# VectorE's evacuation moved ahead of the reciprocal, and the second head mixing run three steps behind the first, in a talking-heads attention with an MLP behind it

## Chip, cores and metric

One core of a Trainium2 chip runs the whole program. The metric is the device time of one launch in microseconds (us); the median of three runs is compared. The core has five engines that work side by side, each through its own instructions in order: TensorE (PE, its weight loads are PEld), VectorE (DVE), ScalarE (ACT), GpSimd (POOL) and SyncE (SP), which here only issues DMA transfers. They wait for one another by semaphores.

## The reference

```python
scores = scale * np.matmul(q, k.transpose(0, 1, 3, 2))        # 4 batches, 12 heads, 448 x 448
scores = np.einsum('bhij,hg->bgij', scores, w_pre)             # first mixing of the heads
scores = scores - np.max(scores, axis=-1, keepdims=True)
attn = np.exp(scores)
attn = attn / (np.sum(attn, axis=-1, keepdims=True) + 1e-09)
attn = np.einsum('bhij,hg->bgij', attn, w_post)                # second mixing
x = np.matmul(attn, v)                                         # -> 1792 tokens x 768
h = x @ w_in                                                   # 768 x 2048
r = np.maximum(h, 0.0)
out = (s * (r * r) + b) @ w_out                                # 2048 x 768
```

## The kernel before

**Blocks and steps.** The queries of a batch are cut into 4 chunks, 16 chunks in all, and each chunk into 11 or 12 blocks of up to 10 queries. A block holds 10 queries x 12 heads = 120 partitions by 448 keys, so that mixing the heads is one matrix product with a 120 x 120 matrix. There are 180 blocks, and one loop over steps `s` (lines 755 to 784) works on several blocks at once, each at another stage.

**What a step does, in the order in which it is written.** `relayout(s + 5)` fetches a block's scores by DMA, and `split(s + 2)` cuts them on GpSimd into a high and a low part. From step 12 on, `convert_step` issues one of the seven VectorE instructions that turn a piece of the MLP's weights into two float parts; seven such pieces are made during the attention, which is 49 steps, 12 to 60. `normalize(s - 1)` takes the reciprocal of the sums (VectorE, L566) and writes the high half of the normalized weights, tile `eh`, on ScalarE (L568). `low_parts()` issues the VectorE subtractions (L233) that are queued in the list `later`. `evacuate(s - 3)` copies the second mixing's result from PSUM (tile `po`) to tile `A` (VectorE L606, ScalarE L604 in the last chunk). `premix(s)` is three matmuls into `pm` (L547), the row maximum (VectorE L549), the exponential with its sum (ScalarE L554) and a small scaling of the sum (ScalarE L558). `remainder(s - 1)` is VectorE L575: the low half of `eh`. `postmix(s - 2)` is the second mixing, twelve matmuls (L590) with `eh` as weights.

**The work between.** A plan that is made ahead (lines 616 to 691) hands each step some of the other work: `prep_q` and `prep_k` (transposes on PE, a copy on ScalarE L443 or L423, and a subtraction for `low_parts`), `qk_pair` (scores of two heads: six matmuls L464, one ScalarE copy L474), `av_pair` (attention times v, L488), loads of q, k and v, and, in the last chunk, pieces of the MLP's first product (`head_piece`, L248). `FILL`, `QK_COST` and `AV_COST` spread the pairs over the steps. A step carries a `prep`, a `qk_pair`, an `av_pair`, both pairs, or nothing. No `qk_pair` stands in a step with a `prep`. In the last chunk (blocks 168 to 179) `split_x` gives six steps a ScalarE copy (L224) and a VectorE subtraction of the MLP's input.

**What keeps the stages apart.** Tiles have a fixed number of buffers: `pm` three PSUM banks together with `px` (two in the last chunk), `po` two, `eh` two, `Tk` (the transposed keys) eight. After step 182 comes the MLP, which the change doesn't touch.

Of the kernel before, what the change touches and what calls it, by code (L numbers as in the profile page):

```python
# [21 lines left out]
def talking_heads_attention__then__act_relu2_kernel(  # L22
# [160 lines left out]
    def convert_step(upto):  # L183

        if done["run"] is None:
            if done["conv"] >= min(upto, len(units)):
                return False
            done["run"] = conversion(done["conv"])
        try:
            next(done["run"])  # L190
        except StopIteration:
            done["run"] = None
            done["conv"] += 1
        return True
# [216 lines left out]
    def prep_k(b, p):  # L411
        low_parts()
        nat = nat_t.pop((b, p))
        tr = bank(f"trk_{b}_{p}") if b == 0 else ps.tile([P, 2, 512], F32, tag="sc", name=f"trk_{b}_{p}")[:, 0]
        for c in range(NC):
            n = P if c < NC - 1 else KL
            nc.tensor.transpose(
                tr[:, c * P:c * P + n],
                nat[:n, c].rearrange("p h d -> p (h d)"),
                ident[:n, :n],  # L420
            )
        t = qkp.tile([P, 2, S], F32R, tag="Tk", name=f"Tk_{b}_{p}", bufs=8)
        nc.scalar.activation(t[:, 0, :], tr[:, :S], AF.Copy)  # L423
        later.append((t[:, 1, :], tr[:, :S], t[:, 0, :]))
        k_t[b, p] = t
# [136 lines left out]
    def normalize(t):  # L562

        n = blocks[t][2] * H
        e, st = e_t[t]
        nc.vector.reciprocal(st[:n, 3:4], st[:n, 2:3])  # L566
        eh = blkp.tile([BP, 2, S], F16, tag="eh", name=f"eh_{t}", bufs=2)
        nc.scalar.activation(eh[:n, 0, :], e[:n], AF.Copy, scale=st[:n, 3:4])  # L568
        eh_t[t] = eh

# [75 lines left out]
            fill.append((when, lo, w1 - 1, QK_COST, 1, qk_pair, (ci, p)))  # L646
    for ci in range(NCH):
        b = chunks[ci][0]
        w0 = first[ci + 1] + 3
        w1 = first[ci + 2] + 3 if ci + 2 <= NCH else NB + 100  # L650
        if ci == NCH - 1:
            w0 = NB + 3
        for p in range(NP):
            when = w0 + p * min(w1 - w0, 12) / NP
            fill.append((when, w0, w1 - 1, AV_COST, 1, av_pair, (ci, p)))
            if b + 1 < B and chunks[ci + 1][0] != b:
                at(w0 + (p + 1) * (w1 - w0) / NP, 2, load_v, b + 1, p)
    w0 = first[NCH - 1] + 3
    for i in range(NHEAD * NKC):
        if i < NHEAD * NKC - LATE:  # L660
            when = w0 + i * (NB + 3 - w0) / (NHEAD * NKC - LATE)
            fill.append((when, w0, NB + 2, 0.567, 1, head_piece, ()))
        else:
            fill.append((NB + 100, NB + 3, NB + 100, 0.567, 1, head_piece, ()))
    fill.sort(key=lambda x: x[0])
    spent, closed = 0.0, {}
    for s in range(NB + 4):
        spent = max(spent, -0.4) + load.get(s, 0)
        left, held = [], set()
        for x in fill:  # L670
            _, lo, hi, cost, order, f, args = x
            waits = f in held

            opens = f is qk_pair or (f is av_pair and args[1] % 4 == 0)
            if opens and closed.get(f, -1) >= s and s <= NB + 2 and s < hi:
                waits = True

            if f is qk_pair and s in load and s < hi:
                waits = True
            if not waits and lo <= s and (s > NB + 2 or hi <= s or (x[0] < s + 4 and spent < FILL)):  # L680
                at(s, order, f, *args)
                spent += cost
                if f is qk_pair or (f is av_pair and args[1] in (3, NP - 1)):
                    closed[f] = s
            else:
                held.add(f)
                left.append(x)
        fill = left
        spent -= FILL
# [62 lines left out]
        x[3](*x[4])  # L752
        low_parts()
    tail = first[NCH - 1]
    for s in range(NB + 3):
        if s == tail - LD:
            early.close()
            rp = ctx.enter_context(tc.tile_pool(name="rp", bufs=1, side="right", reuse_waits="tile"))
            for n in range(NU_EARLY, NU_EARLY + NU_TAIL):
                w_pool[n] = rp  # L760
        if s + LD < NB:
            relayout(s + LD)
        if s + LS < NB:
            split(s + LS)
        if 0 <= s - 1 < NB:
            if s >= CONV0:
                convert_step(NU_EARLY)
            normalize(s - 1)
        low_parts()
        if 0 <= s - 3 < NB:  # L770
            evacuate(s - 3)
        if s < NB:
            premix(s)
        if 0 <= s - 1 < NB:
            remainder(s - 1)
        run_plan(s, True)
        if 0 <= s - 2 < NB:
            postmix(s - 2)
        run_plan(s, False)
        if 0 <= s - (tail - LD) < NKC:  # L780
            load_x(0, 0, s - (tail - LD))
        if 0 <= s - tail < NKC:
            split_x(0, 0, s - tail)
            load_x(0, 1, s - tail)
# [100 lines left out]
```

## Time and profile before

| | |
|---|---|
| median of three runs | 1003.28 us (1002.81 to 1005.6) |
| the profiled execution | 1006.37 us, its span 1004.7 us |
| busy share PE / PEld / DVE / ACT / POOL | 94% / 80% / 64% / 61% / 39% |
| mean granted TensorE clock | 0.98 |
| attention / MLP | up to about 520 us / from there on |

The span is what lies between the first and the last instruction on the core; 1.7 us of the execution lie around it. The chain of waits gives, at each moment, the work that the end hung on; over the span it goes 52% through PE, 21% through ACT and 18% through DVE. Most of PE's share is the MLP.

### The profile page before, as it was taken

The page shows a single profiled execution, that of the slowest core. Times are in us where ns is not written, and L with a number is a line of the kernel's source. Part 1 is how long each engine was busy: PE and PEld are TensorE (multiplying, and loading weights), DVE is VectorE, ACT ScalarE, POOL GpSimd, SP SyncE. Part 2 cuts the span into 40 slices and gives each one's busy share as a digit, 9 for nine tenths or more (in the row PEclk, how much of TensorE's full clock was granted, in tenths as well). Part 3 has the DMA queues.
Part 4 walks back from the last instruction along what each step waited for, and adds up shares of the span by engine and source line. Part 5 has one row for each costly group of instructions (what it writes and reads, how often), then busy time and mean ns, then how long its engine had stood idle before and what let it go on. Part 6 is the DMA issues. An engine that isn't in the chain of part 4 may idle for free.

```text
span 1004.7 us, 19819 instructions
## 1 busy us (share of the span) xinstructions
PE 942.6 (94%) x7500; PEld 799.3 (80%) x7500; DVE 641.9 (64%) x1314; ACT 608.1 (61%) x1315; POOL 393.8 (39%) x458
## 2 busy tenths in 40 slices
PE   5699999989999999999897999899999999999998
PEld 3466677767777677777686999799999899999998
DVE  2679999967877778888636704918542931757411
ACT  2477788868887788887666788612214687821000
POOL 0376667666677566767512333200001333310000
PEclk9889999999999999999798999899999999999999
DMA  3655444664346543544411412314450240145521
GB/s 85 163 134 134 122 144 126 171 158 119 107 121 154 146 129 99 143 126 137 150 30 47 150 56 71 95 63 137 139 177 31 92 142 1 48 126 182 158 95 55
DMA packets 127922, 114.63 MB, mean 114 GB/s; under 512 B 66770, under 2 KB 123730, under 8 KB 127826
## 3 DMA queue, kind: packets, MB, share of 16 engines
q1 hardware_dynamic: 119762, 102.35, 36.8%
q10 hardware_dynamic: 8064, 11.01, 3.0%
q8 instruction: 59, 0.97, 0.4%
q14 instruction: 37, 0.30, 0.1%
HBM read 58.28 MB, written 16.52 MB: 74 GB/s over the span
## 4 chain that ended last, share of the span: by engine, by line
PE 52%; ACT 21%; DVE 18%; DMA 4%; issue 2%; SPq 2%; POOL 0%; ACTq 0%; DVEq 0%; POOLq 0%
PE po L300 23%; PE ph L248 16%; ACT pm L554 7%; ACT S L474 5%; DVE st L549 4%; PE xp L488 4%; PE pm L547 3%; DVE A L606 3%; ACT eh L568 3%; PE sc L464 3%; ACT st L558 2%; PE po L590 2%; DMA blk<-S 2%; DVE eh L575 2%; DVE Tq L233 1%
## 5 line engine op out<-in xcount | busy, mean ns | idle before, releaser
L300 PE MATMUL po<-w,g 128*128 128x384 f32 x1344 | 237.2, 339 | 5.4 <-ACT h L256 5.4
L300 PEld LDWEIGHTS po<-w,g 128*128 128x128 f32 x1344 | 236.2, 190 | 6.0 <-ACT h L256 6.0
L535 POOL TENSOR_TENSOR hl<-blk,hl 120x448 fp32r<-120x448 f32 x180 | 206.8, 1149 | 15.0
L266 POOL TENSOR_TENSOR g<-h,g 128x448 fp32r<-128x448 f32 x64 | 79.1, 1237 | 303.6 <-ACT g L265 291.9
L534 POOL TENSOR_SCALAR hl<-blk 120x448 fp32r<-120x448 f32 x180 | 104.3, 579 | 176.9 <-PE pm L547 131.8
L248 PE MATMUL ph<-x,w 128*128 128x448 f32 x810 | 166.2, 365 | 0.0
L590 PEld LDWEIGHTS <-eh 120*128 120x128 f16 (+1 forms) x2160 | 118.0, 99 | 55.6 <-DVE eh L575 26.0
L248 PEld LDWEIGHTS ph<-x,w 128*128 128x128 f32 x810 | 152.0, 188 | 12.1
L590 PE MATMUL po<-wpost,eh 120*128 120x120 f16 (+1 forms) x2160 | 148.2, 220 | 10.1 <-DVE eh L575 9.9
L554 ACT ACTIVATE pm<-pm,st 120x448 f32<-120x448 f32 x180 | 109.6, 609 | 79.2 <-DVE st L549 78.1
L575 DVE SCALAR_TENSOR_TENSOR eh<-pm,st,eh 120x448 f16<-120x448 f32 x180 | 122.2, 679 | 14.4 <-ACT eh L568 10.5
L549 DVE TENSOR_REDUCE st<-pm 120x1 f32<-120x448 f32 x180 | 111.0, 617 | 15.2 <-PE pm L547 14.6
L568 ACT ACTIVATE eh<-pm,st 120x448 f16<-120x448 f32 x180 | 114.2, 634 | 10.4 <-DVE st L566 10.2
L606 DVE COPY A<-po 128x480 f32<-128x480 f32 x168 | 107.4, 639 | 0.0
L547 PE MATMUL pm<-hl,wpre_hi 120*120 120x448 f32 x360 | 104.2, 371 | 1.2 <-POOL hl L535 1.2
L464 PE MATMUL sc<-Tk,Tq 64*110 64x448 f32 (+1 forms) x576 | 87.4, 412 | 13.7 <-DVE Tk L233 4.8
L488 PE MATMUL xp<-A,v 128*64 128x110 f32 (+1 forms) x1536 | 93.0, 267 | 1.0 <-ACT xs L502 1.0
L154 ACT ACTIVATE mk<-raw 128x384 f32<-128x384 f32 x64 | 35.4, 553 | 95.8 <-DMA raw<-in_moe_w_out_dram 34.0
L474 ACT ACTIVATE S<-sc 110x896 f32<-110x896 f32 (+1 forms) x90 | 82.0, 911 | 13.6 <-PE sc L464 10.1
L488 PEld LDWEIGHTS xp<-A,v 128*64 128x64 f32 x1536 | 75.4, 138 | 16.0 <-issue 8.9
L547 PE MATMUL pm<-hl,wpre_lo 120*120 120x448 f32 x180 | 84.0, 467 | 3.6 <-DVE eh L575 3.1
L547 PEld LDWEIGHTS pm<-hl,wpre_hi 120*120 120x120 f32 x360 | 66.9, 186 | 6.3 <-POOL hl L535 2.0
(64 smaller groups left out, 968.6 us busy)
## 6 DMA issues: line engine op xcount, KB each, us to landing
blk<-S SPq DMA_DIRECT2D x172, 210.0 KB
raw<-in_moe_w_in_dram SPq DMA_DIRECT2D x32, 384.0 KB
raw<-in_moe_w_out_dram SPq DMA_DIRECT2D x32, 384.0 KB
xraw<-xd SPq DMA_DIRECT2D x48, 224.0 KB
part<-ob ACTq DMA_DIRECT2D x28, 192.0 KB
acc<-part SPq DMA_DIRECT2D x28, 192.0 KB
out_dram<-acc ACTq DMA_DIRECT2D x28, 192.0 KB
nk<-in_k_dram SPq DMA_DIRECT2D x48, 96.0 KB
```

The lines of the kernel that those rows point to most:

```text
L248: nc.tensor.matmul(ph[:, :S], w[:, i, c0:c0 + P], x[:, y, :], start=(kc == 0 and m == 0), stop=(kc == NKC - 1 and m == 2),)
L300: nc.tensor.matmul(po[:, :NO], g[:, x, c0:c0 + P], w[:, y, :], start=(f == 0 and m == 0), stop=(f == NF - 1 and m == 2),)
L474: nc.scalar.activation(s_t[ci][:n, 2 * p:2 * p + 2, :], x_t["two"][:n, :, :S], AF.Copy, scale=SCALE)
L488: nc.tensor.matmul(xp[e * D:(e + 1) * D, p % 4, :n], vt[:, e, c, :], a[:, c, 2 * p + e, :n], start=(c == 0), stop=(c == NC - 1),)
L535: nc.gpsimd.tensor_tensor(out=hl[:n, 1, :], in0=blk[:n], in1=hl[:n, 0, :].bitcast(F32), op=ALU.subtract)
L547: nc.tensor.matmul(pm[:n, :S], w[:n, :n], hl[:n, x, :], start=(m == 0), stop=(m == 2))
L549: nc.vector.tensor_reduce(out=st[:n, 0:1], in_=pm[:n, :S], axis=AX.X, op=ALU.max, negate=True)
L554: nc.scalar.activation(e[:n], e[:n], AF.Exp, bias=st[:n, 0:1], accum_out=pm[:n, S:S + 1])
L568: nc.scalar.activation(eh[:n, 0, :], e[:n], AF.Copy, scale=st[:n, 3:4])
L575: nc.vector.scalar_tensor_tensor(out=eh[:n, 1, :], in0=e[:n], scalar=st[:n, 3:4], in1=eh[:n, 0, :], op0=ALU.mult, op1=ALU.subtract,)
L590: nc.tensor.matmul(po[:, c * BP:(c + 1) * BP], eh[:n, x, j0:j0 + P], wpost[:n, y].rearrange("p g i -> p (g i)"), start=(m == 0), stop=(m = ...
L606: nc.vector.tensor_copy(dst, src)
```

## The change

VectorE's order within a step changes. `low_parts` and `evacuate` now stand ahead of `normalize`, so that the reciprocal of a block comes behind the copy to `A`, and the row maximum follows the reciprocal directly. `convert_step` moves from the head of the step to behind `remainder`. `postmix` works on block `s - 3` in place of `s - 2`, and `evacuate` on `s - 4` in place of `s - 3`. The loop has one more step, `eh` a third buffer, and `Tk` seven buffers in place of eight. In the plan, all `av_pair`s and the loads of v that hang on them come one step later, and the head pieces start at the last chunk's fourth step at the earliest.

```diff
-        t = qkp.tile([P, 2, S], F32R, tag="Tk", name=f"Tk_{b}_{p}", bufs=8)
+        t = qkp.tile([P, 2, S], F32R, tag="Tk", name=f"Tk_{b}_{p}", bufs=7)
...
-        eh = blkp.tile([BP, 2, S], F16, tag="eh", name=f"eh_{t}", bufs=2)
+        eh = blkp.tile([BP, 2, S], F16, tag="eh", name=f"eh_{t}", bufs=3)
...
-        w0 = first[ci + 1] + 3
+        w0 = first[ci + 1] + 4
...
-            when = w0 + i * (NB + 3 - w0) / (NHEAD * NKC - LATE)
-            fill.append((when, w0, NB + 2, 0.567, 1, head_piece, ()))
+            when = w0 + i * (NB + 4 - w0) / (NHEAD * NKC - LATE)
+            lo = first[NCH - 1] + max(4, 2 + min(i, NKC - 1))
+            fill.append((when, lo, NB + 3, 0.567, 1, head_piece, ()))
...
-    for s in range(NB + 3):
+    for s in range(NB + 4):
...
+        low_parts()
+        if 0 <= s - 4 < NB:
+            evacuate(s - 4)
         if 0 <= s - 1 < NB:
-            if s >= CONV0:
-                convert_step(NU_EARLY)
             normalize(s - 1)
-        low_parts()
-        if 0 <= s - 3 < NB:
-            evacuate(s - 3)
         if s < NB:
             premix(s)
         if 0 <= s - 1 < NB:
             remainder(s - 1)
+            if s >= CONV0:
+                convert_step(NU_EARLY)
         run_plan(s, True)
-        if 0 <= s - 2 < NB:
-            postmix(s - 2)
+        if 0 <= s - 3 < NB:
+            postmix(s - 3)
```

On VectorE, two steps in a row around blocks 23 to 26, where weights are converted (the rows on `u`, `w` and `raw`). The number behind a name is the block's. Before:

```order
L575 SCALAR_TENSOR_TENSOR eh_23_1369<-pm_23_1333,st_23_1337,eh_23_1369 120x448
L178 SCALAR_TENSOR_TENSOR w_1_1150<-raw_1_330,u_1_1152 128x384
L566 RECIPROCAL st_24_1377<-st_24_1377 120x1
L606 COPY A_2_1382<-po_22_1383 128x48x10
L549 TENSOR_REDUCE st_25_1420<-pm_25_1416 120x1
L575 SCALAR_TENSOR_TENSOR eh_24_1413<-pm_24_1373,st_24_1377,eh_24_1413 120x448
L155 TENSOR_SCALAR u_2_1463<-raw_2_1098 128x384
L566 RECIPROCAL st_25_1420<-st_25_1420 120x1
```

The same engine and blocks in the changed kernel:

```order
L575 SCALAR_TENSOR_TENSOR eh_23_1356<-pm_23_1318,st_23_1322,eh_23_1356 120x448
L176 TENSOR_SCALAR u_1_1142<-w_1_1140 128x384
L606 COPY A_1_909<-po_21_1368 128x48x10
L566 RECIPROCAL st_24_1362<-st_24_1362 120x1
L549 TENSOR_REDUCE st_25_1402<-pm_25_1398 120x1
L575 SCALAR_TENSOR_TENSOR eh_24_1396<-pm_24_1358,st_24_1362,eh_24_1396 120x448
L178 SCALAR_TENSOR_TENSOR w_1_1140<-raw_1_330,u_1_1142 128x384
L606 COPY A_2_1410<-po_22_1411 128x48x10
```

The copy to `A` went from behind the reciprocal to ahead of it, so that only the row maximum (L549) stands between a block's reciprocal (L566) and its remainder (L575).

On VectorE in a step that follows a `prep` (here of `Tq`, line L233). Before:

```order
L159 SCALAR_TENSOR_TENSOR u_2_1463<-raw_2_1098,u_2_1463 128x384
L566 RECIPROCAL st_26_1474<-st_26_1474 120x1
L233 TENSOR_TENSOR Tq_4_1492<-trq_4_0_1493,Tq_4_1492 128x4x110
L606 COPY A_2_1382<-po_24_1479 128x48x10
L549 TENSOR_REDUCE st_27_1522<-pm_27_1518 120x1
```

In the changed kernel:

```order
L155 TENSOR_SCALAR u_2_1452<-raw_2_1088 128x384
L233 TENSOR_TENSOR Tq_4_1468<-trq_4_0_1469,Tq_4_1468 128x4x110
L606 COPY A_2_1410<-po_23_1455 128x48x10
L566 RECIPROCAL st_26_1474<-st_26_1474 120x1
L549 TENSOR_REDUCE st_27_1507<-pm_27_1503 120x1
```

The subtraction and the copy both stand ahead of the reciprocal now.

On PE, the matmuls between two second mixings at block 27. Before:

```order
L439 MATMUL trq_4_0_1493<-ident_124,nq_4_1205 128x110 x4
L488 MATMUL xp_1_0_1446<-A_1_891,v_0_1_404 64x110 x8
L547 MATMUL pm_27_1518<-hl_27_1406,wpre_lo_126 120x448
L547 MATMUL pm_27_1518<-hl_27_1406,wpre_hi_125 120x448 x2
L590 LDWEIGHTS eh_25_1467
```

In the changed kernel:

```order
L439 MATMUL trq_4_0_1469<-ident_124,nq_4_1182 128x110 x4
L488 MATMUL xp_1_0_1475<-A_1_909,v_0_0_400 64x110 x8
L488 MATMUL xp_1_0_1475<-A_1_909,v_0_1_404 64x110 x8
L547 MATMUL pm_27_1503<-hl_27_1391,wpre_lo_126 120x448
L547 MATMUL pm_27_1503<-hl_27_1391,wpre_hi_125 120x448 x2
L590 LDWEIGHTS eh_24_1396
```

The second mixing behind block 27's first takes block 24 in place of 25.

## Rows read from the trace of the kernel before

**Rows 1.** Busy time of each engine in three stretches: the conversion steps, the later attention, and ten microseconds of the last chunk. Columns: stretch in us, its length, then busy us (number of instructions) of PE, PEld, DVE, ACT and POOL, granted TensorE clock, DMA share, GB/s.

```profile
80.00:210.00 130.00, 121.83 (x1352) 89.77 (x1350) 119.35 (x254) 102.92 (x249) 85.94 (x103) 1.00 0.53 142
235.00:470.00 235.00, 228.67 (x2566) 169.85 (x2566) 188.23 (x393) 191.79 (x463) 158.69 (x197) 1.00 0.47 126
480.00:490.00 10.00, 6.88 (x51) 5.38 (x48) 7.41 (x15) 6.88 (x18) 3.86 (x5) 0.61 0.56 177
```

**Rows 2.** Groups of instructions in 80 to 210 us, VectorE. Columns: line, engine, operation, tiles, shapes, count, busy us and mean ns of one, then the idle time of the engine just before them and what ended it.

```profile
L575 DVE SCALAR_TENSOR_TENSOR eh<-pm,st,eh 120x448 f16<-120x448 f32 (+1 forms) x48 | 32.6, 678 | 3.2 <-ACT eh L568 2.5
...
L566 DVE RECIPROCAL st<-st 120x1 f32<-120x1 f32 (+1 forms) x48 | 7.6, 159 | 3.4 <-ACT st L558 3.1
```

**Rows 3.** The same view of 235 to 470 us: the reciprocal, and PE's second mixing.

```profile
L590 PE MATMUL po<-wpost,eh 120*128 120x120 f16 (+1 forms) x1104 | 74.0, 217 | 2.4 <-DVE eh L575 2.3
...
L566 DVE RECIPROCAL st<-st 120x1 f32<-120x1 f32 (+1 forms) x92 | 15.1, 164 | 31.9 <-ACT st L558 31.9
```

**Rows 4.** Timeline of one step that carries neither a `prep` nor a pair (470.67 to 472.95 us), VectorE and ScalarE. Columns: start us, length us, engine, line, operation, tiles, shapes, count, idle time before it and what ended it.

```profile
470.67 0.16 DVE L566 RECIPROCAL st<-st 120x1 f32<-120x1 f32 x1 [0.44 <-ACT st L558]
470.75 0.64 DVE L606 COPY A<-po 128x480 f32<-128x480 f32 x1
470.93 0.63 ACT L568 ACTIVATE eh<-pm,st 120x448 f16<-120x448 f32 x1 [0.29 <-DVE st L566]
...
471.31 0.62 DVE L549 TENSOR_REDUCE st<-pm 120x1 f32<-120x448 f32 x1
...
471.84 0.68 DVE L575 SCALAR_TENSOR_TENSOR eh<-pm,st,eh 120x448 f16<-120x448 f32 x1
471.95 0.61 ACT L554 ACTIVATE pm<-pm,st 120x448 f32<-120x448 f32 x1 [0.39 <-DVE st L549]
...
472.66 0.26 ACT L558 ACTIVATE st<-pm,tiny 120x1 f32<-120x1 f32 x1
...
472.95 0.16 DVE L566 RECIPROCAL st<-st 120x1 f32<-120x1 f32 x1 [0.44 <-ACT st L558]
```

**Rows 5.** Timeline of VectorE in a conversion step, and of one place where the remainder waited for ScalarE's half of `eh`.

```profile
147.17 0.64 ACT L568 ACTIVATE eh<-pm,st 120x448 f16<-120x448 f32 x1
...
147.84 0.69 DVE L575 SCALAR_TENSOR_TENSOR eh<-pm,st,eh 120x448 f16<-120x448 f32 x1 [0.23 <-ACT eh L568]
...
152.52 0.68 DVE L575 SCALAR_TENSOR_TENSOR eh<-pm,st,eh 120x448 f16<-120x448 f32 x1
...
153.12 0.55 DVE L168 SCALAR_TENSOR_TENSOR w<-mk,u 128x384 fp32r<-128x384 f32 x1
...
153.58 0.16 DVE L566 RECIPROCAL st<-st 120x1 f32<-120x1 f32 x1
```

**Rows 6.** Timeline of a step with a `prep_q` (four pairs of heads), VectorE and ScalarE.

```profile
197.46 0.62 DVE L549 TENSOR_REDUCE st<-pm 120x1 f32<-120x448 f32 x1
...
198.12 0.61 ACT L554 ACTIVATE pm<-pm,st 120x448 f32<-120x448 f32 x1 [0.50 <-DVE st L549]
...
198.98 0.56 ACT L443 ACTIVATE Tq<-trq 128x472 fp32r<-128x472 f32 x1
...
199.57 0.65 DVE L233 TENSOR_TENSOR Tq<-trq,Tq 128x472 fp32r<-128x472 f32 x1 [0.29 <-ACT Tq L443]
...
200.14 0.65 DVE L606 COPY A<-po 128x480 f32<-128x480 f32 x1
...
200.70 0.61 DVE L549 TENSOR_REDUCE st<-pm 120x1 f32<-120x448 f32 x1
```

**Rows 7.** Timeline of ScalarE in a step with a `qk_pair`.

```profile
306.77 0.61 ACT L554 ACTIVATE pm<-pm,st 120x448 f32<-120x448 f32 x1
...
307.64 0.91 ACT L474 ACTIVATE S<-sc 110x896 f32<-110x896 f32 x1
...
308.44 0.64 ACT L568 ACTIVATE eh<-pm,st 120x448 f16<-120x448 f32 x1
...
309.06 0.61 ACT L554 ACTIVATE pm<-pm,st 120x448 f32<-120x448 f32 x1
```

**Rows 8.** Timeline of the last chunk, a step with `split_x`, and PE's wait behind it.

```profile
479.67 0.57 ACT L224 ACTIVATE x<-xraw 128x448 fp32r<-128x448 f32 x1
...
480.27 0.69 DVE L233 TENSOR_TENSOR x<-xraw,x 128x448 fp32r<-128x448 f32 x1 [0.30 <-ACT x L224]
480.88 0.64 DVE L606 COPY A<-po 128x480 f32<-128x480 f32 x1
...
482.79 0.70 PE L547 MATMUL pm<-hl,wpre_lo 120*120 120x448 f32 x1 [2.57 <-DVE eh L575]
```

**Rows 9.** Who waited for whom, over the whole span. Columns: waiter, releaser, us in total, times, longest us.

```profile
PE po L590 <- DVE eh L575: 9.9, 21, 1.0
```

**Rows 10.** Timeline, VectorE's row maximum L549: of its 180 instructions, those of blocks 12, 64, 66, 158 and 171 (that of block 61 is the last of Rows 6).

```profile
70.15 0.61 DVE L549 TENSOR_REDUCE st<-pm 120x1 f32<-120x448 f32 x1
...
208.46 0.62 DVE L549 TENSOR_REDUCE st<-pm 120x1 f32<-120x448 f32 x1
...
216.97 0.62 DVE L549 TENSOR_REDUCE st<-pm 120x1 f32<-120x448 f32 x1 [1.25 <-PE pm L547]
...
455.02 0.61 DVE L549 TENSOR_REDUCE st<-pm 120x1 f32<-120x448 f32 x1
...
487.50 0.62 DVE L549 TENSOR_REDUCE st<-pm 120x1 f32<-120x448 f32 x1
```

More of the change, by code (lines that the diff above doesn't have):

```diff
@@ L648, in talking_heads_attention__then__act_relu2_kernel @@
         b = chunks[ci][0]
-        w0 = first[ci + 1] + 3
-        w1 = first[ci + 2] + 3 if ci + 2 <= NCH else NB + 100
+        w0 = first[ci + 1] + 4
+        w1 = first[ci + 2] + 4 if ci + 2 <= NCH else NB + 100
         if ci == NCH - 1:
-            w0 = NB + 3
+            w0 = NB + 4
         for p in range(NP):
@@ L660, in talking_heads_attention__then__act_relu2_kernel @@
         if i < NHEAD * NKC - LATE:
-            when = w0 + i * (NB + 3 - w0) / (NHEAD * NKC - LATE)
-            fill.append((when, w0, NB + 2, 0.567, 1, head_piece, ()))
+            when = w0 + i * (NB + 4 - w0) / (NHEAD * NKC - LATE)
+            lo = first[NCH - 1] + max(4, 2 + min(i, NKC - 1))
+            fill.append((when, lo, NB + 3, 0.567, 1, head_piece, ()))
         else:
-            fill.append((NB + 100, NB + 3, NB + 100, 0.567, 1, head_piece, ()))
+            fill.append((NB + 100, NB + 4, NB + 100, 0.567, 1, head_piece, ()))
     fill.sort(key=lambda x: x[0])
     spent, closed = 0.0, {}
-    for s in range(NB + 4):
+    for s in range(NB + 5):
         spent = max(spent, -0.4) + load.get(s, 0)
@@ L674, in talking_heads_attention__then__act_relu2_kernel @@
             opens = f is qk_pair or (f is av_pair and args[1] % 4 == 0)
-            if opens and closed.get(f, -1) >= s and s <= NB + 2 and s < hi:
+            if opens and closed.get(f, -1) >= s and s <= NB + 3 and s < hi:
                 waits = True
@@ L679, in talking_heads_attention__then__act_relu2_kernel @@
                 waits = True
-            if not waits and lo <= s and (s > NB + 2 or hi <= s or (x[0] < s + 4 and spent < FILL)):
+            if not waits and lo <= s and (s > NB + 3 or hi <= s or (x[0] < s + 4 and spent < FILL)):
                 at(s, order, f, *args)
```

## The prediction

> **What bounds the kernel now.** I read the busy times by stretch first, then the timeline of single steps. Between 80 and 210 us VectorE is busy 119.35 of 130 us and PE 121.83; between 235 and 470 us PE is busy 97% and VectorE 80% [rows 1]. By busy shares PE would set the later stretch. The timeline says something else: most steps have the same length, whatever PE has in them. In a step without filler, the reciprocal comes every 2.28 us, and this is a closed chain: reciprocal to copy 0.08, copy to row maximum 0.56, row maximum to exponential 0.64, exponential to the small scaling 0.71, scaling to the next reciprocal 0.29 [rows 4]. A step with a `prep_q` takes 3.24 us from row maximum to row maximum, through exponential, Tq copy, subtraction, copy to A and row maximum [rows 6]. A step with a `qk_pair` takes 2.29 us, and there ScalarE runs without a gap: exponential, scaling, S copy, eh, exponential [rows 7]. So the attention is held by a chain over VectorE and ScalarE, with PE's own work hardly shorter. The reader is to see that the 0.44 us before each reciprocal [rows 4] lie in that chain, and sum to 31.9 us over 92 steps in the later stretch but only to 3.4 us over 48 conversion steps, where a conversion instruction fills the gap [rows 2, 3].
>
> **The changed order, as chains.** The durations are those above; only who follows whom is new. The copy leaves the chain through the reciprocal and fills VectorE's wait for the exponential. But now only the row maximum stands between a reciprocal and the remainder that needs ScalarE's eh made from it. Reciprocal to eh is 0.26 us [rows 4], eh to the waiting remainder 0.67 [rows 5], together 0.93; reciprocal and row maximum fill 0.08 + 0.53 of that [rows 4]. So each step gets a new wait of 0.32 us on VectorE, and behind it, in order, are queued the conversion instruction, the low parts, the next copy and the next reciprocal.
> The new loop without filler is 0.26 + 0.67 + remainder to next 0.60 [rows 5] + copy 0.56 [rows 4] = 2.09 us, against 2.28: a gain of 0.19. With a conversion instruction of 0.46 (the one of 0.55 us, start to start, [rows 5]) it is 2.55, where the old order needs 2.28 at least (VectorE's own work is 0.08 + 0.56 + 0.53 + 0.60 + 0.46 = 2.23). With a `qk_pair` it stays 2.29, since ScalarE has the same instructions in the same order. In a step with a `prep`, subtraction and copy now stand ahead of the reciprocal, and the chain goes reciprocal to eh 0.26, eh to exponential 0.62 [rows 7], to the Tq copy 0.86, to the subtraction 0.59, to the copy 0.57, to the reciprocal 0.56 [rows 4, 6]: 3.46 against 3.24. For the narrow half of `prep_q` I take 3.0 against 2.8, an estimate by half of the copy's and the subtraction's length.
>
> **The change part by part.**
> *Conversion steps 12 to 60.* By the plan these 49 steps are 11 with a wide `prep`, 4 with a narrow one, 34 others. They take 200.70 - 70.15 = 130.55 us now [rows 6, 10]. After: 34 x 2.55 + 11 x 3.46 + 4 x 3.0 = 136.8 us, **+6.2 us**. Bounds: if VectorE could be packed without any gap, its idle 130 - 119.35 = 10.65 us would go [rows 1], a gain; if the new wait came on top of all that is there, 49 x 0.32 = +15.7. The rows of single steps are the nearest, so I take +6.2.
> *Steps 61 to 157.* These 97 are 20 wide, 9 narrow, 53 with a `qk_pair`, 15 others, and take 455.02 - 200.70 = 254.3 us [rows 6, 10]. Their chains sum to 20 x 3.24 + 9 x 2.8 + 68 x 2.28 = 245.0 now and to 20 x 3.46 + 9 x 3.0 + 53 x 2.29 + 15 x 2.09 = 249.0 after. The other 9.3 us are stalls: 3.0 lie in two steps around 210 us (216.97 - 208.46 = 8.51 where 5.52 were due) [rows 10], which I leave; 6.3 are places where PE and the chain wait for each other. The second mixing's third step gives PE more room, so I keep half of these: 249.0 + 3.0 + 3.1 = 255.1, **+0.8 us**; bounds -5 (all of the 6.3 gone, and the prep steps hidden) and +4.0 (none gone).
> Here the row and a rule can be weighed: PE's matmuls are busy 228.67 of 235 us and its weight loads 169.85 [rows 1]. The Trainium skill (Perfetto Trace Analysis, Identifying the Most-Contended Engine) says that matmul busy time is a poor measure of how full TensorE is, and that the share of weight loads is a better one. By matmul time, 97%, this term could only be the 6.3 us of PE's idle time, a gain, and the sum would be near +1; by weight loads, 72%, PE has room and the chain's +0.8 stands.
> *The last chunk.* From block 158 to 171 it is 32.48 us now [rows 10]. Two `qk_pair` steps of 2.29, eight of 2.09 or a little more and three with `split_x` give the same: the last are 0.26 + 0.62 + 0.86 + 0.60 + 0.61 + 0.56 = 3.51 us each [rows 4, 6 to 8], since the subtraction of x too now stands ahead of the reciprocal; 4.6 + 17 + 10.5 = 32.1. But the copy stays on VectorE for one step more, and head pieces and the last `av_pair`s come a step later, so PE has less to do in the 3.5 us steps. PE waited 2.57 us there [rows 8], and the granted clock was 0.61, the lower level of 1.2 GHz for most of that stretch [rows 1]. At most one step is lost, 3.5 us; I take **+1.5 us**, range 0 to 4.
> *Start and end.* One step more holds no more work; the last second mixings have head pieces beside them on PE, which cover it, and without that cover it is one mixing and its wait, under 2 us. **0**, between -1.5 and +1.
> *Edits at nothing.* `eh` is freed by the mixing one step later and has one buffer more. `Tk` with seven: by the plan, the last `qk_pair` on a tile stands at least a step ahead of the `prep_k` that needs the eighth; if one waited it would cost a step of 2.29 us. On SP, loads of v now share a step with loads of k at two steps near 60; it is in the 3.0 us that I left, and one more such wait would be as long again. The conversion's ScalarE part moves from ahead of eh to behind the scaling, in seven steps, beside VectorE's work.
> **Sum:** +6.2 + 0.8 + 1.5 + 0 = +8.5 us on an execution of 1006.37 (span 1004.7 and 1.7 around it), 1014.9. This one execution lies 3.1 above the median of 1003.28, so the median should be about **1012**, its own range 1003 to 1021: the ends of the terms don't all come together.
>
> **The rivals.**
> *PE sets the time, and its slack is what counts.* With the second mixing a step later, PE no longer waits for a remainder: 9.9 us [rows 9]. For it: PE is 94 to 97% busy in both stretches. Against it: step lengths of 2.28 and 3.24 us that don't follow PE's work. It decides if VectorE's new loop is shorter than PE's mean step in the conversion stretch, 2.55 us or less including preps; my chains give 136.8 / 49 = 2.79. Time: 1003.3 - 9.9 = 993. Chance 0.19.
> *The waits change places and nothing else.* The 0.32 us are hidden as far as the old gaps were, 3.4 + 3.2 us [rows 2], and the later stretch gains what the conversion loses. Time: 1003, within 3 us. Chance 0.10.
> *The change does not do what it says:* seven `Tk` buffers or the loads of v hold a `prep_k` in each of the twelve places. 12 x 2.29 = 27 us more, 1030. Against it: the order in the plan. Chance 0.03.
>
> **How the numbers follow.** The forecast has the rest, 0.68, of which 0.03 lie within the 0.3%, 3.0 us, that a measurement of this kernel can tell from no change. So slower 0.65 + 0.03 = 0.68, same 0.10 + 0.03 = 0.13, faster 0.19. The range goes from 999 to 1021: it leaves out most of the first rival below and 0.03 above.
>
> **What would show it.** In the profile after, the wait of the reciprocal for the scaling (L566) should be almost gone and that of the remainder for eh (L575) stand near 0.3 us a step, some 45 us in all. Steps without filler should take 2.09 us, conversion steps 2.55, `prep` steps 3.46, and the stretch from block 12 to 61 about 137 us. PE's wait for the remainder should fall well under 9.9 us without a gain in time. The forecast is wrong if the conversion stretch stays at 130 us: then the remainder doesn't wait, or PE's work covers it.

## The result, and the profile after

The changed kernel takes 1017.93 us (median; 1015.91 to 1018.25), the kernel before 1003.92 us beside it (1002.81 to 1005.6): a ratio of 1.0131, 95% interval 1.0119 to 1.0143. It is slower, by 14.0 us. Its profiled execution took 1017.73 us with a span of 1016.0 us, 11.3 us more than before. The two differ because the profiled execution of the kernel before, 1006.37 us, lay 2.5 us above its median. The stretches below are read from one execution of each kernel, so they leave 1 to 5 us of a kernel's distance in time to the kernel before without a place.

The row maximum (L549) of a block marks its step, as in [rows 10]. These are the marks of blocks 12, 61, 109, 112, 158, 171 and 179 in the changed kernel, from the timeline of VectorE:

```profile
69.51 0.62 DVE L549 TENSOR_REDUCE st<-pm 120x1 f32<-120x448 f32 x1
...
208.80 0.60 DVE L549 TENSOR_REDUCE st<-pm 120x1 f32<-120x448 f32 x1
...
333.06 0.62 DVE L549 TENSOR_REDUCE st<-pm 120x1 f32<-120x448 f32 x1
...
347.53 0.60 DVE L549 TENSOR_REDUCE st<-pm 120x1 f32<-120x448 f32 x1
...
464.65 0.62 DVE L549 TENSOR_REDUCE st<-pm 120x1 f32<-120x448 f32 x1 [0.28 <-PE pm L547]
...
497.16 0.60 DVE L549 TENSOR_REDUCE st<-pm 120x1 f32<-120x448 f32 x1
...
521.04 0.62 DVE L549 TENSOR_REDUCE st<-pm 108x1 f32<-108x448 f32 x1 [0.67 <-PE pm L547]
```

Differences of such marks give the table by which every kernel of this study is read (us, one profiled execution each; e1 to e12 are the experiments below):

| kernel | blocks 12–61 | 61–109 | 109–112 | 112–158 | 158–179 | 179 to the end | span |
|---|---|---|---|---|---|---|---|
| before | 130.55 | 128.00 | 8.64 | 117.68 | 56.05 | 493.6 | 1004.7 |
| after | 139.29 | 124.26 | 14.47 | 117.12 | 56.39 | 495.0 | 1016.0 |
| e1 later mixing and plan, old order | 132.08 | 128.61 | 11.32 | 119.47 | 56.52 | 494.9 | 1014.3 |
| e2 new order alone | 135.99 | 124.64 | 9.26 | 117.45 | 54.92 | 493.5 | 1006.4 |
| e3 after, conversion ahead of remainder | 132.23 | 127.19 | 12.91 | 118.58 | 56.45 | 496.8 | 1014.7 |
| e4 after, loads of v as before | 139.05 | 124.17 | 13.32 | 117.45 | 56.86 | 495.5 | 1015.9 |
| e5 after, xd stores from ScalarE | 142.40 | 124.68 | 9.92 | 118.46 | 56.81 | 496.6 | 1018.5 |
| e6 another order, lag of two | 149.38 | 127.36 | 7.49 | 121.08 | 55.18 | 494.1 | 1025.5 |
| e7 e6, xd stores from ScalarE | 144.75 | 130.35 | 7.44 | 121.72 | 55.57 | 495.6 | 1026.0 |
| e8 e7's order, lag of three | 144.92 | 126.66 | 8.74 | 118.80 | 56.19 | 496.8 | 1021.9 |
| e9 new plan alone | 133.63 | 126.61 | 11.68 | 118.09 | 55.75 | 494.5 | 1011.3 |
| e10 later mixing, old plan | 132.17 | 126.84 | 8.56 | 118.11 | 54.73 | 495.3 | 1006.4 |
| e11 new order from step 61 on | 130.67 | 125.66 | 9.31 | 117.45 | 55.42 | 493.2 | 1002.6 |
| e12 e2, conversion ahead of remainder | 135.78 | 123.76 | 9.36 | 116.70 | 54.34 | 495.1 | 1005.9 |

After against before: +8.7 us in the conversion steps, -3.7 behind them, +5.8 in three steps at block 109, +1.4 behind block 179, and the rest within 0.7.

**The new wait is there.** Who waited for whom, over the whole span of the changed kernel (waiter, releaser, us in total, times, longest):

```profile
ACT eh L568 <- DVE st L566: 81.5, 96, 2.3
...
DVE eh L575 <- ACT eh L568: 41.4, 131, 3.9
...
ACT S L474 <- DMA blk<-S: 6.8, 4, 3.0
...
DVE st L566 <- ACT st L558: 3.8, 9, 1.1
```

The remainder (L575) waits 131 times, 41.4 us or 0.32 us each time; the reciprocal's wait for the scaling, 31.9 us in the later stretch alone before [rows 3], is 3.8 us in all. The second mixing's wait for the remainder on PE, 9.9 us before [rows 9], is no longer in the list, and the time rose all the same. The line on `S` has grown: ScalarE waits four times, 6.8 us, for a transfer of a block. In the kernel before it waits once for such a transfer, 0.8 us, and once, near 210 us, 2.1 us for a store:

```profile
ACT S L474 <- DMA xd<-xs: 2.1, 1, 2.1
...
ACT S L474 <- DMA blk<-S: 0.8, 1, 0.8
```

**A conversion step** of the changed kernel on VectorE, reciprocal to reciprocal, from the timeline:

```profile
94.60 0.15 DVE L566 RECIPROCAL st<-st 120x1 f32<-120x1 f32 x1
94.67 0.61 DVE L549 TENSOR_REDUCE st<-pm 120x1 f32<-120x448 f32 x1
95.45 0.68 DVE L575 SCALAR_TENSOR_TENSOR eh<-pm,st,eh 120x448 f16<-120x448 f32 x1 [0.18 <-ACT eh L568]
96.06 0.55 DVE L159 SCALAR_TENSOR_TENSOR u<-raw,u 128x384 uint32<-128x384 uint32 x1
96.52 0.65 DVE L606 COPY A<-po 128x480 f32<-128x480 f32 x1
97.09 0.15 DVE L566 RECIPROCAL st<-st 120x1 f32<-120x1 f32 x1
```

It is 2.49 us long, and the only gap is the remainder's. A step without filler, that of block 166, two steps ahead of the last chunk; the two ACT rows are ScalarE's `eh` and exponential:

```profile
482.04 0.16 DVE L566 RECIPROCAL st<-st 120x1 f32<-120x1 f32 x1
482.11 0.61 DVE L549 TENSOR_REDUCE st<-pm 120x1 f32<-120x448 f32 x1
482.29 0.64 ACT L568 ACTIVATE eh<-pm,st 120x448 f16<-120x448 f32 x1 [0.60 <-DVE st L566]
482.82 0.60 ACT L554 ACTIVATE pm<-pm,st 120x448 f32<-120x448 f32 x1
482.95 0.68 DVE L575 SCALAR_TENSOR_TENSOR eh<-pm,st,eh 120x448 f16<-120x448 f32 x1 [0.24 <-ACT eh L568]
483.56 0.65 DVE L606 COPY A<-po 128x480 f32<-128x480 f32 x1
484.12 0.15 DVE L566 RECIPROCAL st<-st 120x1 f32<-120x1 f32 x1
```

It takes 2.08 us from reciprocal to reciprocal, against 2.28 in [rows 4]: the same order that costs in a conversion step pays here.

**The place that no term had.** Three steps at block 109 took 5.8 us more. ScalarE there, from the timeline; the number in brackets is its idle time and what ended it:

```profile
332.28 0.26 ACT L558 ACTIVATE st<-pm,tiny 120x1 f32<-120x1 f32 x1
335.59 0.92 ACT L474 ACTIVATE S<-sc 118x896 f32<-118x896 f32 x1 [3.05 <-DMA blk<-S]
336.40 0.62 ACT L502 ACTIVATE xs<-xp,xscale 128x440 f32<-128x440 f32 x1
336.92 0.64 ACT L568 ACTIVATE eh<-pm,st 120x448 f16<-120x448 f32 x1
```

The first scores of chunk 11 go into the buffer that held those of chunk 9 (`S` has two), and a transfer to a block of chunk 9 had not yet read it. Behind this copy stand `eh` and, through it, the remainder, which waited 3.9 us there; PE waited 2.9 us for the copy. SP, which issues these transfers, in the changed kernel:

```profile
303.20 0.81 SPq L527 DMA_DIRECT2D blk<-S  x1
308.06 0.38 SPq L507 DMA_DIRECT2D xd<-xs  x1
308.53 0.81 SPq L527 DMA_DIRECT2D blk<-S  x1
...
318.47 0.54 SPq L507 DMA_DIRECT2D xd<-xs  x1
...
326.66 2.70 SPq L390 DMA_DIRECT2D nk<-in_k_dram  x2
...
331.46 1.76 SPq L527 DMA_DIRECT2D blk<-S  x2
```

and in the kernel before, the same two stores of chunk 7's result (`xd`), a transfer behind them, and the same copy on ScalarE, which did not wait:

```profile
290.26 0.82 SPq L527 DMA_DIRECT2D blk<-S  x1
295.97 0.38 SPq L507 DMA_DIRECT2D xd<-xs  x1
...
306.49 0.39 SPq L507 DMA_DIRECT2D xd<-xs  x1
...
324.08 0.82 SPq L527 DMA_DIRECT2D blk<-S  x1
...
328.17 0.92 ACT L474 ACTIVATE S<-sc 118x896 f32<-118x896 f32 x1
```

SP stands at the first store until the `av_pair`s have made its data: 4.0 us after, 4.9 us before. But in the changed kernel the store comes 12 us later (308.06 against 295.97). About 5 us of this are the lateness that the changed kernel already had (block 96's mark stands at 300.9 against 295.9). The other 7 are three steps, and these come from the plan: worked through for both kernels, it puts the fourth `av_pair` of chunk 7, on which the store hangs, at step 98 in place of 95. So the `av_pair`s don't all come one step later, as the section on the change has it: 66 of the 96 do, 14 come two steps later, four come three steps later and 12 not at all; 14 of the 84 `qk_pair`s come a step later too.

From this store on SP issues without a pause in both kernels until the scores are due. The last transfer out of chunk 9, block 111's by the order of the transfers, goes out at 324.08 us before, 4.1 us ahead of the copy; in the changed kernel it goes out at 331.46, 1.1 us before ScalarE is free for the copy (332.54).

The granted clock fell there too, and in the conversion steps. The changed kernel in windows of 10 us (us, length, busy us of PE, PEld, DVE, ACT, POOL, granted clock, DMA share, GB/s):

```profile
80.00:90.00 10.00, 7.33 (x65) 5.15 (x62) 8.91 (x20) 5.90 (x16) 4.42 (x5) 0.80 0.27 68
...
330.00:340.00 10.00, 5.75 (x59) 4.39 (x60) 5.47 (x13) 4.73 (x12) 6.14 (x7) 0.93 0.60 145
340.00:350.00 10.00, 10.00 (x88) 7.26 (x85) 6.16 (x14) 6.80 (x17) 3.65 (x5) 0.73 0.53 134
```

PE, 5.75 us busy in the ten with the wait, is busy without a break in the next ten, at a mean clock of 0.73, partly at the lower of its two levels (1.2 GHz). The first row is a place in the conversion steps: PE waited there for a low part,

```profile
86.78 1.47 PE L464 MATMUL sc<-Tk,Tq 64*118 64x448 f32 x6 [1.95 <-DVE Tk L233]
```

and the step behind it, from block 18's mark to block 19's, took 4.09 us against 2.28 before. In 180 to 190 us the clock was 0.83, and the two steps from block 53's mark took 6.9 us against 5.4. The kernel before has 1.00 in all four windows.

### The profile page after: what moved, and what is told of

Same layout as the page of the kernel before. It is cut to its first block, busy times and chain, and to the rows that moved or that the text cites. A ratio compares the mean times of both kernels' runs of the same rounds, so it can differ in the third digit from the quotient of the medians.

```text
span 1016.0 us, 19954 instructions
## 1 busy us (share of the span) xinstructions
PE 946.1 (93%) x7500; PEld 802.6 (79%) x7500; DVE 640.4 (63%) x1314; ACT 603.2 (59%) x1315; POOL 392.7 (39%) x458
## 4 chain that ended last, share of the span: by engine, by line
PE 62%; ACT 15%; DVE 12%; DMA 5%; issue 2%; SPq 2%; POOL 1%; ACTq 0%; DVEq 0%; POOLq 0%
PE po L300 23%; PE ph L248 16%; PE pm L547 7%; PE xp L488 5%; PE po L590 5%; ACT eh L568 4%; PE sc L464 4%; DMA blk<-S 3%; ACT pm L554 3%; DVE A L606 3%; ACT S L474 2%; DVE eh L575 2%; ACT st L558 1%; DVE raw L172 1%; DVE Tk L233 1%
## 5 line engine op out<-in xcount | busy, mean ns | idle before, releaser
L590 PEld LDWEIGHTS <-eh 120*128 120x128 f16 (+1 forms) x2160 | 120.1, 101 | 43.2 <-issue 40.7
L590 PE MATMUL po<-wpost,eh 120*128 120x120 f16 (+1 forms) x2160 | 150.3, 221 | 1.6 <-DVE A L606 1.6
L575 DVE SCALAR_TENSOR_TENSOR eh<-pm,st,eh 120x448 f16<-120x448 f32 x180 | 122.9, 683 | 43.6 <-ACT eh L568 41.4
L549 DVE TENSOR_REDUCE st<-pm 120x1 f32<-120x448 f32 x180 | 110.1, 612 | 25.5 <-PE pm L547 25.0
L464 PEld LDWEIGHTS sc<-Tk,Tq 64*110 64x110 f32 (+1 forms) x576 | 47.2, 184 | 37.2 <-ACT S L474 12.4
```

The source lines that it names most:

```text
L464: nc.tensor.matmul(sc[e][:n, :S], qt[r0:r0 + D, p, x, :n], kt[r0:r0 + D, y, :], start=(m == 0), stop=(m == 2),)
L549: nc.vector.tensor_reduce(out=st[:n, 0:1], in_=pm[:n, :S], axis=AX.X, op=ALU.max, negate=True)
L575: nc.vector.scalar_tensor_tensor(out=eh[:n, 1, :], in0=e[:n], scalar=st[:n, 3:4], in1=eh[:n, 0, :], op0=ALU.mult, op1=ALU.subtract,)
L590: nc.tensor.matmul(po[:, c * BP:(c + 1) * BP], eh[:n, x, j0:j0 + P], wpost[:n, y].rearrange("p g i -> p (g i)"), start=(m == 0), stop=(m = ...
```

## The experiments

Each was timed against the kernel before on the same chip, but not all on one chip, so experiments are compared by their ratios. Stretches are those of the table above.

**e1: the later mixing and its plan, with VectorE's old order.**

```diff
+        if 0 <= s - 1 < NB:
+            if s >= CONV0:
+                convert_step(NU_EARLY)
+            normalize(s - 1)
         low_parts()
         if 0 <= s - 4 < NB:
             evacuate(s - 4)
-        if 0 <= s - 1 < NB:
-            normalize(s - 1)
```

(and no `convert_step` behind the remainder)

> The changed kernel with VectorE's old order within the step (conversion, reciprocal, low parts, copy to A), so that only the later second mixing and what hangs on it (plan, buffers, loads) is left of the change. Theory A (the new order's wait of the remainder costs the conversion steps, the loads on SP cost the stall near block 110): steps of 2.28 and 3.2 us as before, blocks 12 to 61 in about 130 us, the stall near block 110 stays, some 4 us more at the end; about 1010 us. Theory B (the later second mixing itself is the loss): as the changed kernel, 1018 us.

Measured: 1015.94 us, ratio 1.0094 (1.0074 to 1.0115). Neither theory's time came. The conversion steps are near their old length, as theory A had it, but most of the loss is there without the new order: +2.7 us at 109–112, +1.8 at 112–158, +1.5 in the conversion steps, +1.3 each ahead of block 12 and behind block 179.

**e2: the new order alone, in the kernel before** (lag of two, old plan, old buffers).

```diff
-        if 0 <= s - 1 < NB:
-            if s >= CONV0:
-                convert_step(NU_EARLY)
-            normalize(s - 1)
         low_parts()
         if 0 <= s - 3 < NB:
             evacuate(s - 3)
+        if 0 <= s - 1 < NB:
+            normalize(s - 1)
...
             remainder(s - 1)
+            if s >= CONV0:
+                convert_step(NU_EARLY)
```

> The kernel before with VectorE's new order alone (low parts and copy ahead of the reciprocal, conversion behind the remainder); second mixing, plan and buffers as before. Theory A: blocks 12 to 61 in about 138 us, wait of the remainder for eh about 40 us in all, other steps without filler 2.05, no stall near block 110; about 1009 us. Theory B: no loss without the later mixing, 1004 us or less.

Measured: 1008.68 us, ratio 1.0034 (1.0022 to 1.0046). This is theory A. The conversion steps lose 5.4 us, blocks 61–109 gain 3.4: the order loses where a conversion instruction is queued behind the remainder's wait, and gains where none is. Whether that wait is the price here, with a lag of two, e12 tests. The order's 0.34% and e1's 0.94% add up to about the 1.31% of the whole.

**e3: the changed kernel with the conversion instruction ahead of the remainder,** where VectorE else waits for `eh`.

```diff
         if 0 <= s - 1 < NB:
-            remainder(s - 1)
             if s >= CONV0:
                 convert_step(NU_EARLY)
+            remainder(s - 1)
```

> The changed kernel with the conversion instruction between the row maximum and the remainder in place of behind the remainder. Theory A: the instruction lies in the new wait of 0.3 us, so conversion steps without a prep fall from 2.5 to about 2.25 us and blocks 12 to 61 from 139 to about 130 us; about 1009 us. Theory B: no change, 1018 us.

Measured: 1016.3 us, ratio 1.010 (1.0084 to 1.0116). The conversion steps fall from 139.3 to 132.2 us, so with a lag of three the wait was their price, as theory A had it; theory A's time, 1009, did not come. Of these 7.1 us the span keeps 1.3 (the ratios differ by 0.3%, about 3 us): 1.0 us is lost ahead of block 12, 2.9 between 61 and 109, 1.5 at 112–158 and 1.8 behind block 179, while 109–112 gains 1.6. Of the 7.1 us, 1.2 lie in the two steps from block 53's mark, where e3's clock did not fall.

**e4: the changed kernel with the loads of v at their old steps.**

```diff
-                at(w0 + (p + 1) * (w1 - w0) / NP, 2, load_v, b + 1, p)
+                at(w0 - 1 + (p + 1) * (w1 - w0) / NP, 2, load_v, b + 1, p)
```

> The changed kernel with the loads of v in the steps in which the kernel before has them, one step earlier, so that they no longer share a step with loads of k. Theory A (the 5.8 us between blocks 109 and 112 are a wait of the S copy for late block transfers that stand behind those loads on SP): blocks 109 to 112 in about 9 us, near 1012 us. Theory B (the transfers are late for another reason): 14 us there as in the changed kernel, 1018 us.

Measured: 1020.02 us, ratio 1.014 (1.0116 to 1.0163). The stall at 109–112 stays, 13.3 us, theory B: the loads of v are not its cause.

**e5: the changed kernel with the stores of `xd` issued by ScalarE,** so that SP can't stand at them.

```diff
-            nc.sync.dma_start(
+            nc.scalar.dma_start(
                 xd[b][p0:p + 1, :, n0:n0 + n].rearrange("a p n -> p a n"), xs[:, p0:p + 1, :n]
```

> The changed kernel with the stores of the attention's output (xd) issued by ScalarE, which has just written them, in place of SP. Theory A (the later av_pairs let SP stand at a store, and the loads of k and v and the block transfers behind it come too late for the S copy): no S copy waits for a block transfer any more, blocks 109 to 112 take 9 to 10 us in place of 14.5, 153 to 155 some 2 us less; about 1011 us. Theory B (the issues of v, k and blocks alone fill SP): the stall stays within 1 us, 1017 us or more.

Measured: 1020.72 us, ratio 1.0153 (1.0132 to 1.0175). The stall is nearly gone (9.9 us at 109–112, where the kernel before has 8.6), and no `S` copy waits for a transfer there, so SP's standing at the store made it. The time is no better: 3.1 us more in the conversion steps, 1.3 at 112–158 and 1.6 behind block 179. The trace of e5 shows a part of it on ScalarE, here just behind the place of the stall:

```profile
345.42 0.45 ACT L502 ACTIVATE xs<-xp,xscale 128x220 f32<-128x220 f32 x1
348.00 0.40 ACTq L507 DMA_DIRECT2D xd<-xs  x1
348.45 0.63 ACT L568 ACTIVATE eh<-pm,st 120x448 f16<-120x448 f32 x1 [2.58 <-DMA nq<-in_q_dram]
```

ScalarE now stands at the store itself, and the step from block 112's mark takes 3.72 us in place of 2.20. Behind every store the next instruction of ScalarE begins at least 0.44 us after the copy to `xs`; in the changed kernel it begins 0.1 us before the copy's end at 15 of 31 such places. Four of these lie in the conversion steps, which makes about 2 of the 3.1 us there, an estimate. The rest is not settled.

**e6, e7, e8: another order,** copy to `A`, reciprocal, row maximum, conversion instruction, low parts, remainder; e6 with a lag of two and the old plan, e7 the same with the `xd` stores on ScalarE, e8 as e7 with the changed kernel's lag and plan.

```diff
-        if 0 <= s - 1 < NB:
-            if s >= CONV0:
-                convert_step(NU_EARLY)
-            normalize(s - 1)
-        low_parts()
         if 0 <= s - 3 < NB:
             evacuate(s - 3)
+        if 0 <= s - 1 < NB:
+            normalize(s - 1)
         if s < NB:
             premix(s)
+        if 0 <= s - 1 < NB and s >= CONV0:
+            convert_step(NU_EARLY)
+        low_parts()
         if 0 <= s - 1 < NB:
             remainder(s - 1)
```

> The kernel before (second mixing two steps behind, its plan and buffers) with VectorE's copy ahead of the reciprocal as in the change, but the conversion instruction and the low parts between the row maximum and the remainder, where the new wait lies. Theory A (the wait of the remainder is the price of the new order, the later second mixing buys nothing): wait of the remainder under 15 us, blocks 12 to 61 in 124 to 128 us, steps after a prep about 2.7 us; about 997 us. Theory B (the third step of the second mixing is needed for a gain): PE waits more for the remainder, over 15 us, and the time is 1004 us or more.

> The kernel of e6 with the stores of xd issued by ScalarE. If SP's queue takes back what the faster steps gain, some 3 us less than e6, about 994 us; if not, the same.

> As e7, but on the changed kernel, with the second mixing three steps behind. Theory A: the third step buys nothing and costs 2 to 4 us at the end of the attention, about 997 us, slower than e7. Theory B: with the waits filled, the third step pays, faster than e7.

Measured: e6 1026.46 us, ratio 1.0217 (1.0202 to 1.0232); e7 1030.77, 1.0264 (1.0245 to 1.0284); e8 1024.14, 1.0191 (1.0166 to 1.0215). None comes near the times that were hoped for (997, 994 and 997). e6's theory B has the direction of the time but not the reason: the second mixing on PE waits 9.8 us for the remainder, as before. The waits of e6 show why:

```profile
POOL hl L534 <- PE pm L547: 156.2, 146, 5.3
DVE st L549 <- PE pm L547: 94.9, 108, 4.0
...
PE sc L464 <- DVE Tq L233: 18.2, 18, 2.6
PE sc L464 <- DVE Tk L233: 17.7, 19, 2.1
```

In the kernel before these four are 131.8, 14.6, 3.5 and 4.8 us in all. The low parts (L233) now stand behind the row maximum, which needs PE's first mixing; PE, in order, waits for the low parts ahead of its scores and comes late to the next first mixing. This closes a loop through VectorE and PE that the kernel before does not have. e8 beats e7, its theory B, which shows only that a third step can pay in an order that makes the remainder late.

**e9: the new plan alone, in the kernel before** (`av_pair`s one to three steps later; mixing, order and buffers old).

```diff
-        w0 = first[ci + 1] + 3
-        w1 = first[ci + 2] + 3 if ci + 2 <= NCH else NB + 100
+        w0 = first[ci + 1] + 4
+        w1 = first[ci + 2] + 4 if ci + 2 <= NCH else NB + 100
...
-            fill.append((when, w0, NB + 2, 0.567, 1, head_piece, ()))
+            lo = first[NCH - 1] + max(4, 2 + min(i, NKC - 1))
+            fill.append((when, lo, NB + 2, 0.567, 1, head_piece, ()))
```

> The kernel before, with the plan of the changed one alone: the av_pairs (and the loads of v and the store of the attention's result that hang on them) one step later, the head pieces not before the last chunk's fourth step; the second mixing still runs two steps behind, and VectorE has its old order. Theory A (what the lag cost came from the plan: the av_pairs at other steps move the store on SP's queue behind which the transfers of the next blocks stand): the stall of the later mixing alone is here too, blocks 109 to 112 take 11 us or more in place of 8.6, blocks 153 to 156 some 10 in place of 7.7, and the total is 1009 to 1013 us. Theory B (it came from the mixing itself being a step later): the stretches stay within 1 us of the kernel before, total 1004 us.

Measured: 1013.25 us, ratio 1.0088 (1.0062 to 1.0113), theory A, at its upper end. The stall is there without any later mixing, 11.7 us at 109–112, and so are 3.1 us in the conversion steps, 2.6 of them in the two steps from block 19's mark (8.47 us against 5.83), where the granted clock in 90 to 100 us is 0.83 and 1.00 before. The edit moves the `av_pair`s and, through the plan, 14 `qk_pair`s, so it tests the plan as a whole. ScalarE at block 109 in e9:

```profile
330.33 0.26 ACT L558 ACTIVATE st<-pm,tiny 120x1 f32<-120x1 f32 x1
332.85 0.92 ACT L474 ACTIVATE S<-sc 118x896 f32<-118x896 f32 x1 [2.26 <-DMA blk<-S]
```

**e10: the mirror,** e1 with the `av_pair`s at their old steps (the two lines of e9 back to `+ 3`, the last chunk's excepted).

> The mirror of the plan alone: the later mixing with three buffers of eh, seven of Tk and VectorE's old order, and the av_pairs at the steps of the kernel before (the last chunk's excepted, which can't). Theory A (the plan carried the loss): blocks 109 to 112 take about 8.6 us, the stretch 112 to 158 is as before, 117.7 us, only the end of the attention keeps its 3 to 4 us, total 1007 to 1008 us. Theory B (the later mixing itself): as the lag with its plan, 1015 to 1016 us.

Measured: 1009.35 us, ratio 1.0046 (1.0031 to 1.006). The stall is gone, 8.56 us at 109–112, and block 179 comes at 511.08 us, as before (511.07). Of theory A the place is right and the time some 2 us too low. In the profiled executions the later mixing by itself gains nothing up to block 179 and loses 1.7 us behind it; by the medians it loses 4.6 us, of which the other 2.9 have no place in the table. Theory B's 1015 is refuted.

**e11: the kernel before with the new order only from step 61 on,** behind the conversion.

```diff
-        if 0 <= s - 1 < NB:
+        if 0 <= s - 1 < NB and s < 61:
             if s >= CONV0:
                 convert_step(NU_EARLY)
             normalize(s - 1)
         low_parts()
         if 0 <= s - 3 < NB:
             evacuate(s - 3)
+        if 0 <= s - 1 < NB and s >= 61:
+            normalize(s - 1)
```

> The kernel before with the old order of VectorE up to step 60 and the new one (low parts, copy to A, reciprocal) from step 61 on, where no conversion instruction is left; two steps of lag. Theory A (the order costs only where a conversion instruction stands behind the remainder's new wait): blocks 12 to 61 take 130.5 us as before, blocks 61 to 109 some 124.6 as with the new order throughout, total 1000 to 1001 us. Theory B (what one stretch gains, the next loses, since PE's work and the transfers catch up): total 1003 to 1005 us.

Measured: 1004.07 us, ratio 0.9987 (0.9974 to 1.0). Theory B: the conversion steps are as before, 130.67 us, but blocks 61–109 gain 2.3 us and not 3.4, and the three steps at 109 lose 0.7. It is the fastest kernel of the study beside the one before, and not measurably faster.

**e12: e2 with the conversion instruction ahead of the remainder** (the diff of e3 on e2).

> The kernel before with the new order of VectorE alone (low parts at the head of the step, copy to A, reciprocal, row maximum), and the conversion instruction between the row maximum and the remainder, where VectorE else waits for eh; two steps of lag, old plan. Theory A (the remainder's wait of 0.3 us is the price of the conversion steps, and the conversion instruction can stand in it): blocks 12 to 61 take 128 to 131 us in place of 136, blocks 61 to 109 124.6, total 1000 to 1003 us. Theory B (as with the conversion moved in the changed kernel, most is given back behind block 61 or at its end): 1006 to 1008 us.

Measured: 1007.35 us, ratio 1.0024 (1.0015 to 1.0034). Theory A fails: the conversion steps stay at 135.8 us where e3 had 132.2. Waits in that stretch of e12:

```profile
PEld L590 <- DVE eh L575: 19.3, 29, 1.9
PE po L590 <- DVE eh L575: 9.4, 15, 1.5
```

The remainder no longer waits for `eh`, but it comes later, and with a lag of two the second mixing is already waiting for it; in e3, with a lag of three, neither wait is there in that stretch. So in this order the third step is worth about 3.5 us in the conversion steps. As a whole e3, which has the new plan too, is slower than e12 (1.010 against 1.0024).

## Why the prediction was right in time and half right in its reasons

*The total* (1012, 999 to 1021) holds the 1017.9 us, and slower was its likeliest case: +8.7 us on the median was forecast, +14.0 came. That the time fell inside the range is in part luck. A stall of 5.8 us, which the sum had at nothing, was partly made up by steps that gained where they were to lose.

*The chains.* The new wait was to be 0.32 us a step and some 45 us in all; it is 0.32 and 41.4. Steps without filler were to take 2.09 us and mostly take 1.96 to 2.08 behind block 61, conversion steps 2.55 and mostly take 2.49. A wide `prep` step was to take 3.46 and takes 3.24 to 3.41 in 24 of 31 cases: the chain from `eh` to the exponential was taken as 0.62 us from a step with a `qk_pair`, where ScalarE is full; in the step without filler above it is 0.53, and so it is in the middle over the changed kernel's steps from 200 to 470 us.

*Conversion steps.* Predicted +6.2 us, measured +8.7. The order's own part is +5.4 (e2), near the term. Whose the rest is, isn't settled: the plan alone costs 3.1 us there (e9), the later mixing alone 1.6 (e10), and both together in the old order 1.5 (e1). In the trace of the changed kernel, 3.3 us of the 8.7 lie in the three steps at the two places where the granted clock fell. The wait as the mechanism is shown, for a lag of three, by e3, which fills only that wait and takes 7.1 us back.

*Steps 61 to 157.* Predicted +0.8 us, measured +1.5, as the sum of two misses: up to block 109 the steps gained 3.7 us where I had them losing, and the stall at 109 cost 5.8. The gain isn't in the 15 `prep` steps of that stretch, which rose from 48.5 to 51.1 us, nearly as predicted. It is in the other 33, which fell from 79.5 to 73.2: a step with a `qk_pair` was to stay at 2.29 us, and its median there fell from 2.28 to 2.19. Its sum had the same 0.62, which is shorter in the changed kernel.

*"Edits at nothing".* This is the step that failed. I looked for the loads of v on SP, and priced one more wait like the 3.0 us near 210 without putting it into the sum. e4 shows that the loads of v are innocent. What counts are the `av_pair`s themselves, one to three steps later: the store that hangs on them holds SP until a later time, the transfers of the next blocks are queued behind it, and the first scores of the chunk after next wait for those transfers. e9 has it with the plan alone, e10 loses it with the plan back, e5 loses it when SP doesn't issue the store. As ratios: the plan alone 0.88%, the order alone 0.34%, the later mixing without its plan 0.46%, all together 1.31%. They don't add up, and need not.

*The last chunk* was +1.5 us and is 32.51 against 32.48 to block 171. Start and end, at 0, are -0.6 to block 12 and +1.7 from 171 on; 1.4 of these lie behind block 179, and every kernel with a lag of three has 1.3 us or more there. But e7 and e12, with a lag of two, have 2.0 and 1.5, so it is not settled that the lag makes it.

*The rivals.* "PE sets the time" is refuted in its own terms: the second mixing's wait for the remainder went, and no microsecond came back. In the changed kernel PE's matmuls are busy 116.92 of 120 us and its weight loads 86.66, from 340 to 460 us:

```profile
340.00:460.00 120.00, 116.92 (x1279) 86.66 (x1276) 92.79 (x197) 95.71 (x234) 77.83 (x96) 0.98 0.47 126
```

The Trainium skill (Perfetto Trace Analysis, Identifying the Most-Contended Engine) has the share of weight loads, 72% here, as a better measure than matmul time, 97% here; the trace is in line with it, as taking PE's wait away gained nothing. "The waits change places" holds for e11, behind the conversion, and not for the whole. Seven buffers of `Tk` did no visible harm: e10 has seven, and reaches block 179 when the kernel before does.

*What stays open:* why e5, nearly without the stall, is no faster than the changed kernel, beyond the part that ScalarE's stores show; where the 2.7 us lie by which the medians differ more than the profiled executions; and how a lag of three with the old plan, the new order and e3's conversion would do. By the table its conversion steps should take about 132 us and its other stretches those of e10 and e12, which is near the kernel before. This is an estimate; it was not run.

## What to carry to other kernels

A step that is moved takes its stores with it: find out on which queue they are issued and what stands behind them there, for the price shows several steps later and on another engine. Draw the loop that closes a step, with the order of each engine, before a wait is removed: the reordering moved 0.3 us from one wait to another, which is a gain where VectorE has room and a loss where an instruction is queued behind the new wait. And an extra step of lag is worth something only where the consumer is seen to wait in that very order: here nothing in the kernel before, and 3.5 us in the conversion steps once the remainder was late.

## What was not expected of the hardware

SP's queue was full, though SP does nothing here but issue: a transfer of a block holds it for 0.8 us, a load of k (two parts) for 1.8 to 2.75, and from 308 to 344 us it issued without a pause; in the kernel before too, from 296 us on. The Trainium skill (Perfetto Trace Analysis, DMA Optimizations) says that spreading the issues over several engines may help where the issuing one is the bottleneck; e5 does so for the stores, and agrees as to the stall but not as to the time, since ScalarE then stood at the stores (0.44 us and more each). And one wait cost PE twice: after the 3 us at 332 to 336 the next ten microseconds ran at a granted clock of 0.73 with PE busy throughout, where the kernel before has 1.00 in the same ten.
